# Scaling of q and v moved to the front of GpSimd's work of a step, in a retention layer fused with an x - tanh(x) feed-forward block

## The chip, the cores and the metric

One Trainium2 chip, one of its cores. The metric is the device time of the kernel in microseconds (us), as the median of several runs. Before the change it is 703.7 us (8 runs, 703.37 to 704.32).

## The reference

```python
# attention: q, k, v are (4, 8, 768, 64) f32
gamma = 1.0 - 2.0 ** (-5.0 - np.arange(H, dtype=np.float32))
scale = 1.0 / np.sqrt(D)
for t in range(S):
    state = gamma[None, :, None, None] * state + np.einsum('bhd,bhe->bhde', k[:, :, t], v[:, :, t])
    y[:, :, t] = scale * np.einsum('bhd,bhde->bhe', q[:, :, t], state)
# bridge: (B, H, S, D) -> x of (3072, 512)
# feed-forward: w_in (512, 2048), w_out (2048, 512), float64 as handed in
h = x @ w_in
g = h - np.tanh(h)
out = (g @ w_out).astype(np.float32)
```

## The kernel before, in words

**Attention by chunks.** The 3072 tokens are 24 chunks of 128. The decay gamma is taken out of the recurrence: q is multiplied by gamma^t / sqrt(D) and v by gamma^-t (`scale`, L262, one multiplication of 128x512 each, in place), so that a chunk needs only masked scores and a running state. A chunk ci passes through these pieces:

- `load_chunk` (L245): SP issues the loads of k, q and v, 256 KB each, in this order.
- `scale` (L262): q (which = 0) and v (which = 1).
- `turn_by_dma` (L300 to L305): ScalarE copies k and then the scaled q into `apart`, with the halves of each word apart; a DMA from ScalarE's queue writes that to `rows` in DRAM (L303); a transposing DMA on SP's queue reads it back as `kqT` (L305).
- `products` (L325, L331): PE's state products k, v and scores kqT. Then `mask` (L338) and `state` (L348 to L354) on VectorE.
- `outputs` and `outputs_rest` (L379): PE's y; `see` (L409) and `keep_x` (L425): ScalarE reads it and stores it as xT, the feed-forward's input.

**Feed-forward by steps.** The list `steps` has 96 entries (n, m2): a tile of 256 tokens by 256 hidden columns. Steps are called here by their place in it, from 0. In a step PE makes h (`up`, L444), ScalarE and VectorE make g = h - tanh(h) (`shrink_*`, L454 to L503), and PE multiplies g by w_out (`down`, L511) two steps later, so that h's two banks and the o banks are handed on from step to step. Where a run of steps on the same tokens ends, VectorE or ScalarE adds o into the sum (`add_up`, L521, L525), which frees the o bank for the next run. From step 32 on (n >= 4) a step uses a scheme with fewer products (`fast_up`, L758; `fast_products`, L649), which needs sums of weights and of tokens made ahead by GpSimd: `up_weights` (L738), `up_tokens` (L748), `fast_weights` (L590); and in each of these steps GpSimd adds pairs (`up_pairs`, L768) which VectorE uses in L773.

**Weights.** They come as 64-bit words and are turned into f32 by `convert`: two operations on ScalarE (L177, L178), four on VectorE (L186 to L192), and two on GpSimd (L200 `low` times `power`, L204 the sum, which writes w1 or w2). The buffers of `head`, `low` and `power` are double; `raw` has three.

**What sets the order.** The pools make the buffers, but the order of each engine's work is that of the program text: every engine, SP's queue too, runs its instructions in the order in which the loop issues them. Up to step 7 the order is a list written out by hand (`order`), and the change doesn't touch it. From step 8 the loop below runs. Two of three steps hold a chunk step (`with_chunk`); where it `falls_back` it stands behind that step's `up`. A chunk step ci does products of chunk ci + 2, loads chunk ci + 4 and turns chunk ci + 3 by DMA. `with_weights` gives steps 8 to 26 a conversion (two in step 8), and `with_sums` gives steps 25 to 39 and some later ones their sums. The scaling of the chunk that the next step's chunk step turns is issued in the step ahead of it:

| step | PE starts it, us | chunk step ci | chunk scaled | conversion | sums |
|---|---|---|---|---|---|
| 9 | 99.07 | 5 | none | 14 | |
| 10 | 105.95 | none | 9 | 15 | |
| 11 | 112.93 | 6 | 10 | 16 | |
| 12 | 121.02 | 7, falls back | none | 17 | |
| 17 | 163.33 | 10 | 14 | 22 | |
| 25 | 231.81 | none | 19 | 30 | up_weights 0 |
| 26 | 238.79 | 16 | 20 | 31 | up_weights 1 |
| 27 | 247.86 | 17, falls back | none | none | up_weights 2 |
| 28 | 256.80 | none | 21 | none | up_weights 3 |
| 29 | 264.80 | 18 | 22 | none | up_weights 4 |
| 30 | 273.88 | 19, falls back | none | none | up_weights 5, first tokens |
| 31 | 283.05 | none | 23 | none | up_weights 6 and 7, tokens 5 |
| 32 | 290.03 | 20 | none | none | fast_weights 0 |

The pattern repeats every three steps: chunk scalings stand in steps 8, 10, 11, 13, 14, 16, 17, 19, 20, 22, 23, 25, 26, 28, 29 and 31, for chunks 8 to 23. In steps 11, 14, 17, 20, 23, 26 and 29 the chunk that is scaled is also loaded in the same step.

Of the kernel before, what the change touches and what calls it, by code (L numbers as in the profile page):

```python
# [31 lines left out]
def kernel(  # L32
# [25 lines left out]
    nc = tc.nc  # L58
# [147 lines left out]
    def convert(i):  # L206
        convert_begin(i)
        convert_bits(i)
        convert_end(i, nc.gpsimd)
# [38 lines left out]
    def scale(ci, which, engine):  # L248
        if ci >= NCH:
            return  # L250
        t, g = loaded[ci][1 + which], (gw if ci < WIDE else gq, gv)[which]
        out_ = t
        if which == 0 and ci < WIDE:
            if not wide:
                wide.append(mid.tile([P, 2, RUN, 2, D], F32, tag="apart", name="wide", bufs=1))
            out_ = loaded[ci][1] = wide[0][:, ci % 2]
            out_ = out_.rearrange("p r i d -> p i r d")
            t, g = (x.rearrange("p (i r) d -> p i r d", r=RUN) for x in (
                t, g[:, ts(ci % CPB, H)][:, :, None].to_broadcast([P, H, D])))
        else:  # L260
            g = g[:, ts(ci % CPB, H)][:, :, None].to_broadcast([P, H, D])
        engine.tensor_tensor(out_, t, g, op=ALU.mult)  # L262
# [51 lines left out]
    def products(ci):  # L314

        kh, _, vh = loaded[ci]
        kT, qT = (sides[ci][:, i] for i in range(2))
        sp = banks("t", f"s_{ci}")
        keep_busy(sp[:, 0, :P])
        scores[ci] = halves = sp.rearrange("p r (w n t) -> p r w n t", w=2, n=NP)  # L320
        for p in range(NP):
            for a in range(2):
                for i in range(2):
                    h, r = 2 * p + i, ds(D * a, D)
                    nc.tensor.matmul(halves[ds(D * i, D), a, 1, p], kh[r, h], vh[r, h],  # L325
                                     start=True, stop=True, skip_group_check=True)
        for p in range(NP):
            for a in range(2):
                for i in range(2):
                    r = ds(D * i, D)  # L330
                    nc.tensor.matmul(halves[ds(D * a, D), i, 0, p], kT[r, p, ts(a, D)],  # L331
                                     qT[r, p, ts(a, D)], start=True, stop=True,
                                     skip_group_check=True)

    def mask(ci):
        halves = scores[ci]
        m = mid.tile([P, 2, NP, D], F32, tag="a", name=f"a_{ci}")
        nc.vector.tensor_tensor(m, halves[:, :, 0],  # L338
                                causal[:, None, None, :].to_broadcast([P, 2, NP, D]),
                                op=ALU.mult)  # L340
        masked[ci] = m

    def state(ci):
        halves = scores[ci]
        j = ci % CPB
        if j == 0:
            states[ci] = mid.tile([P, 2, NP, D], F32, tag="state", name=f"state_{ci}", bufs=3)
            nc.vector.tensor_copy(states[ci][:, 1], halves[:, 0, 1])  # L348
        else:
            nc.vector.tensor_tensor(states[ci][:, 1], halves[:, 0, 1], states[ci][:, 0],  # L350
                                    op=ALU.add)
        if j < CPB - 1:
            nxt = mid.tile([P, 2, NP, D], F32, tag="state", name=f"state_{ci + 1}", bufs=3)
            nc.vector.tensor_tensor(nxt[:, 0], halves[:, 1, 1], states[ci][:, 1], op=ALU.add)  # L354
            states[ci + 1] = nxt
# [56 lines left out]
    def outputs_rest(ci):  # L412
        halfway.pop(ci)(False)
        loaded.pop(ci)

    def keep_x(ci):
        n, nj = divmod(ci, BLK)
        if n not in xT:
            for i in (1, 0) if n == 0 else (n,):
                xT[i] = xp.tile([P, NP, BLK * P], F32, tag="xT", name=f"xT_{i}")  # L420

        half = xT[n][:, :, ts(nj // 2, TH)].rearrange("p (n r) t -> p r n t", r=2)
        y = y_banks[:, ci % 2][:, :: 1 - 2 * (ci % 2)]
        for odd in range(2):
            nc.scalar.copy(out=half[:, :, :, ds(P * odd + D * (nj % 2), D)],  # L425
                           in_=y[:, :, :, odd::2])
# [39 lines left out]
    def shrink_factors(n, m2):  # L466
        u = shrinking[n, m2][0]
        if n < FAST_UP:
            shrink_factor(n, m2)
        large, q1 = work("large", 2), work("q1", 1)  # L470
        nc.scalar.activation(q1, u, AF.Square, bias=bias1, scale=math.sqrt(A))  # L471
        nc.scalar.activation(large, u, AF.Relu, bias=bias_m)  # L472
        shrinking[n, m2] += [q1, large]
# [15 lines left out]
    def shrink_last_factor(n, m2):  # L489

        hp = hps.pop((n, m2))
        q1 = shrinking[n, m2][3]
        g = gT[n, m2] = gp.tile([P, 2, TH], F32, tag="g", name=f"g_{n}_{m2}")
        dst = hp if n < FAST_UP else g.rearrange("p i t -> p (i t)")
        nc.vector.scalar_tensor_tensor(dst, in0=q1, scalar=A * C1, in1=hp, op0=ALU.add,  # L495
                                       op1=ALU.mult)
        shrinking[n, m2].append(dst)
# [264 lines left out]
    def up_take(n, m2):  # L762
        nc.scalar.copy(out=odd_room[0], in_=hps[n, m2])  # L763
# [106 lines left out]
    with_chunk = {h // 2: FIRST - 3 + i for i, h in enumerate(halves)}  # L870
# [28 lines left out]
    def middle():  # L899

        if before and len(shrinking[before]) == 2:
            shrink_factor(*before)
            shrink_third(*before)

    def chunk_step(ci):
        if ci >= FIRST:
            outputs_rest(ci)
            keep_x(ci)
        middle()
        if before:  # L910
            shrink_factors(*before)
            shrink_last_factor(*before)
        if FIRST <= ci + 2 < NCH:
            products(ci + 2)
            mask(ci + 2)
            state(ci + 2)
        load_chunk(ci + 4)
        if not before:
            turn_and_see(ci)
        elif FIRST <= ci + 1 < NCH - 1:  # L920
            outputs(ci + 1)

    def turn_and_see(ci):
        if ci + 3 < NCH:
            turn_by_dma(ci + 3)
        if FIRST <= ci + 1 < NCH - 1:
            if not before:
                outputs(ci + 1)
            see(ci + 1)

    for s in range(BEGUN, len(steps)):
        n, m2, first, last = steps[s]
        fast = n >= FAST_UP
        ci = with_chunk.get(s)

        falls_back = s == FALL or s in behind_up
        lag = LAG + int(s >= FALL)
        if ci is not None and not falls_back:
            chunk_step(ci)
        for i in with_weights.get(s, []):  # L940
            convert(i)
            load_weights(i + 3)
        if fast:
            fast_up(n, m2, (1, 5, 7, 6))
            up_take(n, m2)
        else:
            for i in range(2):
                up(n, m2, i)
        if falls_back and ci is not None:
            chunk_step(ci)  # L950
        if before and ci is not None:
            turn_and_see(ci)
        if ci == NCH - 2:
            outputs(ci + 1)
            see(ci + 1)
        waiting.append(steps[s])
        if fast:
            if before and ci is None:
                shrink_factors(*before)
                shrink_last_factor(*before)  # L960
            up_pairs()
            for make in with_sums.get(s, []):
                make()
            downs(lag, 0)
            fast_up(n, m2, (2, 3, 4))
            up_add(n, m2)
            shrink_begin(n, m2)
            if before:
                shrink_end(*before)
                if before[0] >= FAST:  # L970
                    fast_sums(*before)
            downs(lag, 1)
            end_some(1)
            shrink_two(n, m2)
            before = n, m2
            if s + 1 not in with_chunk:
                middle()
        else:
            shrink_begin(n, m2)
            shrink_factors(n, m2)  # L980
            shrink_multiply(n, m2)
            downs(lag)
            shrink_last_factor(n, m2)
            shrink_end(n, m2)
            for make in with_sums.get(s, []):
                make()
        if s + 1 in with_chunk:
            for which in range(2):
                scale(with_chunk[s + 1] + 3, which, nc.gpsimd)
    shrink_factors(*before)  # L990
    shrink_last_factor(*before)
    shrink_end(*before)
# [64 lines left out]
```

## Time and profile before

| | |
|---|---|
| median of 8 runs | 703.7 us |
| the profiled execution, device time | 703.7 us |
| its span in the profile | 701.9 us |
| granted TensorE clock | 0.999 of full |
| PE busy | 690.8 us |
| VectorE (DVE) busy | 520.2 us |
| ScalarE (ACT) busy | 432.8 us |
| GpSimd (POOL) busy | 353.7 us |
| scaling of q on GpSimd from 90 us on (L262) | 16 times, median 1042 ns |
| scaling of v on GpSimd from 90 us on (L262) | 16 times, median 1272 ns |
| L200 on GpSimd, in the whole run | 30 times, median 1278 ns |

How to read it. The span is what the profiler saw of the program; the device time holds what lies around it. An engine is busy while it works on an instruction; PE's ends are modelled. In the view of waits a line names the engine and instruction that stood idle, what ended its idle time, the total, how often and the longest. In the timeline a number in square brackets is the idle time ahead of an instruction and what ended it. The chain of work that ended last is followed back from the program's end, at each step to what released it; "issue" in it is time in which the engine waited for nothing that the profile shows.

### The profile page before, as it was taken

The page shows a single profiled execution, that of the slowest core. Times are in us where ns is not written, and L with a number is a line of the kernel's source. Part 1 is how long each engine was busy: PE and PEld are TensorE (multiplying, and loading weights), DVE is VectorE, ACT ScalarE, POOL GpSimd, SP SyncE. Part 2 cuts the span into 40 slices and gives each one's busy share as a digit, 9 for nine tenths or more (in the row PEclk, how much of TensorE's full clock was granted, in tenths as well). Part 3 has the DMA queues.
Part 4 walks back from the last instruction along what each step waited for, and adds up shares of the span by engine and source line. Part 5 has one row for each costly group of instructions (what it writes and reads, how often), then busy time and mean ns, then how long its engine had stood idle before and what let it go on. Part 6 is the DMA issues. An engine that isn't in the chain of part 4 may idle for free.

```text
span 701.9 us, 16649 instructions
## 1 busy us (share of the span) xinstructions
PE 690.8 (98%) x6602; PEld 579.3 (83%) x6602; DVE 520.2 (74%) x888; ACT 432.8 (62%) x818; POOL 353.7 (50%) x523
## 2 busy tenths in 40 slices
PE   7999999999999999999999999999999999999997
PEld 6886666677667667679999999999999999999996
DVE  4898878979889667676776677676686676776765
ACT  4677657776767675565556655555665555666553
POOL 1464444645445577768854453354453444544333
PEclk9999999999999999999999999999999999999999
DMA  7880437887877666510000000000000000000001
GB/s 211 247 253 28 134 96 206 227 227 185 228 212 187 152 161 185 164 51 1 1 1 16 16 1 16 16 1 31 1 1 31 1 1 31 2 15 16 1 16 46
DMA packets 119677, 59.96 MB, mean 85 GB/s; under 512 B 101808, under 2 KB 112688, under 8 KB 119600
## 3 DMA queue, kind: packets, MB, share of 16 engines
q1 hardware_dynamic: 117008, 50.21, 27.2%
q10 hardware_dynamic: 2592, 8.69, 3.2%
q8 instruction: 52, 0.85, 0.5%
q14 instruction: 25, 0.20, 0.1%
HBM read 35.83 MB, written 14.68 MB: 72 GB/s over the span
## 4 chain that ended last, share of the span: by engine, by line
PE 82%; DVE 5%; ACT 4%; POOL 3%; issue 2%; DMA 2%; SPq 1%; ACTq 0%; POOLq 0%; DVEq 0%
PE h L758 28%; PE o L511 12%; PE h L444 10%; PE fast_t L649 10%; PE y L649 8%; PE fast_o L649 8%; PE y L379 3%; PE s L331 1%; ACT apart L300 1%; PE s L325 1%; POOL low L200 1%; DMA raw<-in_moe_w_in_dram 1%; POOL fast_raw L738 1%; DMA kqT<-rows 1%; DVE g L503 1%
## 5 line engine op out<-in xcount | busy, mean ns | idle before, releaser
L600 POOL TENSOR_TENSOR s<-g 128x128 f32<-128x128 f32 x64 | 29.2, 457 | 191.9 <-DVE g L503 188.0
L457 ACT ACTIVATE th<-h 128x512 f32<-128x512 f32 x64 | 38.2, 597 | 141.3 <-DVE h L775 138.6
L511 PE MATMUL o<-w,g 128*128 128x512 f32 x256 | 116.0, 596 | 0.8 <-DVE sum L521 0.8
L444 PE MATMUL h<-xT,w 128*128 128x256 f32 x480 | 110.2, 382 | 0.0
L444 PEld LDWEIGHTS h<-xT,w 128*128 128x128 f32 x480 | 90.0, 190 | 20.6 <-issue 8.9
L503 DVE COPY_PREDICATED g<-large,th 128x512 f32<-128x512 int32 x96 | 86.2, 898 | 10.0 <-DVE g L502 0.5
L200 POOL TENSOR_TENSOR low<-low,power 128x512 f32<-128x512 f32 x30 | 38.6, 1288 | 107.1 <-DVE power L192 74.3
L511 PEld LDWEIGHTS o<-w,g 128*128 128x128 f32 x256 | 47.5, 190 | 48.5 <-issue 44.0
L758 PEld LDWEIGHTS h<-xT,w 128*128 128x128 f32 x512 | 76.8, 191 | 8.4 <-ACT fast_head L763 1.0
L482 DVE TENSOR_TENSOR th<-h,th 128x512 f32<-128x512 f32 x94 | 64.1, 682 | 22.6 <-ACT th L455 21.3
L758 PE MATMUL h<-xT,w 128*128 128x128 f32 x512 | 78.3, 275 | 0.2 <-ACT fast_head L763 0.2
L773 DVE TENSOR_TENSOR h<-h,fast_head 128x256 f32<-128x256 f32 x64 | 27.7, 432 | 67.0 <-PE h L758 65.9
L463 ACT ACTIVATE q<-u,tab 128x512 f32<-128x512 f32 x96 | 69.7, 726 | 1.8
L495 DVE SCALAR_TENSOR_TENSOR g<-q,h 128x512 f32<-128x512 f32 x64 | 44.0, 688 | 36.0 <-ACT q L471 34.5
L471 ACT ACTIVATE q<-u,tab 128x512 f32<-128x512 f32 x96 | 69.5, 724 | 0.0
L472 ACT ACTIVATE large<-u,tab 128x512 f32<-128x512 f32 x96 | 68.5, 714 | 0.0
L758 PE MATMUL h<-x,w 128*128 128x128 f32 x448 | 68.3, 275 | 0.0
L486 DVE SCALAR_TENSOR_TENSOR h<-q,h 128x512 f32<-128x512 f32 x94 | 64.8, 689 | 3.8 <-ACT q L463 3.8
L758 PEld LDWEIGHTS h<-x,w 128*128 128x128 f32 x448 | 59.0, 192 | 0.0
L763 ACT COPY fast_head<-h 128x512 f32<-128x512 f32 x64 | 37.5, 585 | 20.1 <-PE h L758 20.0
L502 DVE TENSOR_TENSOR g<-g,u 128x512 f32<-128x512 f32 x64 | 49.2, 768 | 0.0
L768 POOL TENSOR_TENSOR fast_head<-fast_head 128x256 f32<-128x256 f32 x64 | 46.8, 731 | 4.5 <-ACT fast_head L763 4.5
(195 smaller groups left out, 1479.3 us busy)
## 6 DMA issues: line engine op xcount, KB each, us to landing
rows<-apart ACTq DMA_DIRECT2D x16, 512.0 KB, 4.0
k<-in_k_dram SPq DMA_DIRECT2D x24, 256.0 KB, 4.0
v<-in_v_dram SPq DMA_DIRECT2D x24, 256.0 KB, 4.6
raw<-in_moe_w_out_dram SPq DMA_DIRECT2D x12, 512.0 KB, 4.2
out_dram<-sum SPq DMA_DIRECT2D x22, 256.0 KB, 2.0
q<-in_q_dram SPq DMA_DIRECT2D x16, 256.0 KB, 4.7
raw<-in_moe_w_in_dram SPq DMA_DIRECT2D x14, 256.0 KB, 3.9
raw<-in_moe_w_in_dram SPq DMA_DIRECT2D x28, 128.0 KB, 3.7
```

Source lines behind the costliest of these rows:

```text
L444: nc.tensor.matmul(hp, w1[:, c, ts(2 * m2 + i, P)], xT[n // 2][:, c, ts(n % 2, TH)], start=(i == 0 and c == 0), stop=(c == NC - 1), skip_g ...
L463: nc.scalar.activation(q0, shrinking[n, m2][0], AF.Square, bias=bias0)
L471: nc.scalar.activation(q1, u, AF.Square, bias=bias1, scale=math.sqrt(A))
L472: nc.scalar.activation(large, u, AF.Relu, bias=bias_m)
L482: nc.vector.tensor_tensor(th, hp, th, op=ALU.subtract)
L486: nc.vector.scalar_tensor_tensor(hp, in0=shrinking[n, m2][2], scalar=C0, in1=hp, op0=ALU.add, op1=ALU.mult)
L502: nc.vector.tensor_tensor(flat, src, u, op=ALU.mult)
L503: nc.vector.copy_predicated(flat, large.bitcast(I32), th)
L511: nc.tensor.matmul(o_p[j], gT[n, m2][:, i, ts(j, P)], w2[:, 2 * m2 + i], start=(first and i == 0), stop=(last and i == 1))
L649: nc.tensor.matmul(accs[n][k], left[k - 1], right, start=first and k in (1, 6, 7, 4), stop=last, skip_group_check=True)
L758: nc.tensor.matmul(hps[n, m2][:, ts(PLACE[k], P)], s_of[m2][k - 1][:, c], x_of[n][k - 1][:, c], start=(k == 1 and c == 0), stop=(c == 1), ...
L768: nc.gpsimd.tensor_tensor(odd_room[1], first[:, :2], first[:, 3:1:-1], op=ALU.add)
```

## The change

The two scalings of the chunk that the next step turns are issued right behind this step's chunk step (or, where it has none or falls back, as the first thing of the step), ahead of the conversion and of the sums; before they were the last thing of the step.

```diff
@@ -937,6 +937,9 @@
         lag = LAG + int(s >= FALL)
         if ci is not None and not falls_back:
             chunk_step(ci)
+        if s + 1 in with_chunk:
+            for which in range(2):
+                scale(with_chunk[s + 1] + 3, which, nc.gpsimd)
         for i in with_weights.get(s, []):
             convert(i)
             load_weights(i + 3)
@@ -984,9 +987,6 @@
             shrink_end(n, m2)
             for make in with_sums.get(s, []):
                 make()
-        if s + 1 in with_chunk:
-            for which in range(2):
-                scale(with_chunk[s + 1] + 3, which, nc.gpsimd)
     shrink_factors(*before)
     shrink_last_factor(*before)
     shrink_end(*before)
```

Each engine but GpSimd has the same instructions in the same order as before; on GpSimd the pairs of L262 stand ahead of L200, L204, L738 and L748 of their step.

## The prediction

> **What bounds the kernel now.** First the busy shares of the page, then who waits for whom on PE from 40 to 330 us (which holds every step that the edit touches), then PE's timeline, then the chain of work that ended last.
>
> ```profile
> PE 690.8 (98%) x6602; PEld 579.3 (83%) x6602; DVE 520.2 (74%) x888; ACT 432.8 (62%) x818; POOL 353.7 (50%) x523
> ```
>
> PE is busy 690.8 of 701.9 us, so an edit on GpSimd (POOL) can pay only by what PE waits. These are all its waits in that stretch (us in total, times, longest):
>
> ```profile
> PE s L331 <- DMA kqT<-rows: 1.0, 1, 1.0
> PE o L511 <- DVE sum L521: 0.8, 1, 0.8
> PE y L379 <- DVE state L348: 0.3, 1, 0.3
> PE h L758 <- ACT fast_head L763: 0.2, 1, 0.2
> ```
>
> The third lies before 92 us, ahead of the edit. The other three in PE's timeline would be at 126.26, 261.17 and 308.16; the first two are these, in steps 12 and 28:
>
> ```profile
> 126.26 0.69 PE L331 MATMUL s<-kqT 64*64 64x64 f32 x32 [1.00 <-DMA kqT<-rows]
> ...
> 261.17 3.70 PE L511 MATMUL o<-w,g 128*128 128x512 f32 x8 [0.75 <-DVE sum L521]
> ```
>
> The chain says what stands behind the first (start, us, what); the q is chunk 9's:
>
> ```profile
> 113.66 1.28 POOL low L200
> ...
> 116.25 1.05 POOL q L262
> ...
> 117.32 1.05 ACT apart L300
> ...
> 118.39 3.62 DMA rows<-apart
> ...
> 122.03 4.18 DMA kqT<-rows
> ...
> 126.26 0.69 PE s L331 x32
> ```
>
> and behind the second, with chunk 20's q after the sums of up_weights (L738):
>
> ```profile
> 254.43 0.72 POOL fast_raw L738
> ...
> 255.15 1.01 POOL q L262
> ...
> 256.19 1.06 ACT apart L300
> ...
> 258.10 0.60 ACT u L454
> ...
> 259.22 0.69 DVE th L482
> ```
>
> Both go through the moved instruction: q is scaled last, ACT's copy of it (L300) waits, and all that ACT has behind it is late. ACT's waits from 90 to 300 us give the total, six waits:
>
> ```profile
> ACT apart L300 <- POOL q L262: 14.4, 6, 3.7
> ```
>
> **What the two waits really cost.** [...] I compare step lengths. Step 12 runs on PE from 121.02 to 131.12, 10.10 us; step 15, alike but for 16 more y matmuls (150.73 to 151.01, 0.28), from 147.18 to 156.35, 9.17. So 10.10 - (9.17 - 0.28) = 1.21 us. Step 28, 256.80 to 264.80, is 8.00; step 22, the same work, 206.58 to 213.56, is 6.98: 1.02 us. Together 2.23 us, where the idle marks say 1.75.
>
> [...] L503 takes 0.73 alone and 1.55 at 173.89 under the q scaling of 173.80, and the v scaling behind it takes 1.51 where 1.04 is its length alone.
>
> **The change, part by part.** Nothing is added or removed: 16 times q (1.04 us) and v (1.04 to 1.5) move ahead of that step's conversion (L200 and L204, 1.28 + 1.27, with about 2.6 from start to end) and sums. No DMA is issued by them and no queue is reordered; SP's list is the same.
>
> Step 10, chunk 9. GpSimd ended conversion 14 at 110.77. Its q load was issued at 101.51; q loads take 4.0 to 6.2 us, so it is there by 107.7. q is then scaled by 111.9, not 117.3. ACT's copy of k starts at 112.98 by ACT's own order, that of q then at 113.95, not 117.32: rows goes out 3.4 us earlier, at 115.0. Its landing (2.6 to 5.3 us) falls at 117.6 to 120.3; SP issues the transposing load after v of chunk 10, at 117.74 or later, and it takes 4.2 to 5.1: kqT is there at 122.0 to 125.4, likeliest (3.6 and 4.2) 122.8. PE wants it at 126.26 - 1.21 = 125.05. Gain 1.21, at worst 0.9.
>
> Step 26, chunk 20. GpSimd is free at 243.06; q's load, issued at 240.31, lands by 244.3 to 246.5; q is done by 247.6, and ACT wants it at 253.5. ACT's wait of 2.65 us goes whole. u, th, L482, L486 and the first L521 (260.43) come 2.65 earlier, at 257.8; PE's o result is there at 256.8. PE wants the bank at 261.17 - 1.02 = 260.15. Gain 1.02, covered by 1.7 us or so.
>
> The other four waits of ACT (3.7, 0.9, 0.7, 3.2 us) end in no PE wait: worth nothing.
>
> What goes behind q and v. In steps 11, 14, 17, 20, 23, 26 and 29 the load is issued in the same step, so GpSimd now stands waiting for it with the conversion queued behind. Step 17: v issued at 165.39, scaled by 173.5 at the latest, L200 2.3 us later than its 171.20, the weights at 176.1; PE wants them in step 19, at 184.80. The nearest case is conversion 31 in step 26: v issued at 240.88, 4.3 to 6.3 us to land, 1.04 to 1.5 to scale: L200 by 248.7, weights by 251.3 (251.68 now), wanted at 253.26 - 1.21 = 252.05. Cost 0, covered by 0.7 us at the worst end. ACT's next use of the head and low buffers is two conversions on: a whole step of cover.
>
> Steps 29 to 32. q of chunk 22 started at 271.31 and v at 273.48, on their loads; 265.79 to 269.30 was up4. Now up4 waits behind v: 3.5 us later. The 1.33 us that GpSimd waited at 285.95 is filled. So it is through with step 31 at 293.18 + 3.5 - 1.33 = 295.35, and up_pairs of step 32 is 0.5 us later than here:
>
> ```profile
> 294.87 0.72 POOL L768 TENSOR_TENSOR fast_head<-fast_head 128x256 f32<-128x256 f32 x1 [1.68 <-ACT fast_head L763]
> ```
>
> VectorE uses it at 297.33, when PE's h is there: 297.33 - 294.87 - 0.72 = 1.7 us of cover. Cost 0; without that cover it is one for one.
>
> Meeting on SBUF. q and v stretch other VectorE operations than before. Now a scaling costs L503 and the next L186 about 0.8 each; after, the loads' arrival decides. I take no difference; bounds -1.6 (no more meetings) and +1.8 us of VectorE in each of the 13 steps that scale and convert (rival D). VectorE is idle 39.5 of 200 us from 92 to 292, and g is ready well ahead (step 21's at 210.65, used at 219.20), which hides it.
>
> Sum: -1.21 - 1.02 = -2.2 us. The profiled execution took 703.7 us with a span of 701.9, and 703.7 is also the median of the eight runs: 703.7 - 2.2 = 701.5.
>
> **Rivals.**
> A. The forecast, 701.5; its own range 701.1 (the third wait, 308.16, goes too: step 34 would gain 0.3) to 702.1 (only the idle marks count).
> B. One wait stays. For: rows now runs beside the loads of chunk 10, and 125.4 is past 125.05; against: that needs both slowest landings. 703.7 - 1.0 to 1.2 = 702.6.
> C. It doesn't do what it says: PE's waits move to the next thing that is just late, and none of 2.2 us comes out: 703.7. For: the chain has DVE and ACT pieces too. Against: 3.4 and 2.65 us of relief for needs of 1.2 and 1.0.
> D. Slower: [...] q now falls on L186 to L192 (the conversion's SBUF operations), and pushes L200 and L204 from under VectorE's PSUM operations (L482 to L502, 2.8 us) onto L503. [...] From 92 to 240 VectorE has 148 - 127.7 = 20.3 us idle; half of it is usable at best when its inputs come in fixed order, plus 8.5 us of lead in g: 18.6. It decides from (18.6 + 2.2) / 13 = 1.6 us more VectorE a step, the gain eaten first. At 1.8, a hit by each of L200 and L204 more than now, it is 23.4 - 18.6 = 4.8 us of PE, less 2.2 gained: 703.7 + 2.6 = 706.3. Against: 1.6 is already paid a step now, and it goes when q moves.
>
> **How the numbers follow.** A 0.62, B 0.15, C 0.09, D 0.14. A measurement here tells about 0.2% (1.4 us) from none, that is below 702.3 or above 705.1. A is faster, B and C are the same, D is slower: faster 0.62, same 0.24, slower 0.14. The range 701.0 to 703.9 holds A (its end of 701.1 and what the median wavers), B and C, and leaves out D.
>
> **What would show it.** Right: no wait of L331 for kqT in step 12 and none of L511 for L521 in step 28; those steps 8.9 and 7.0 us long on PE; ACT's waits for q near 0; rows of chunk 9 out 3 us earlier; GpSimd idle before q, for its load; up_pairs of step 32 about 0.5 us later against PE. Wrong: a new PE wait for L204, for L773 or for g, or VectorE's L503 and L186 to L192 in sum over 1.4 us longer a step.

## The result and the profile after

The median after is 701.86 us (12 runs, 701.33 to 703.01), before 703.71 (32 runs): ratio 0.9974, 95% interval 0.9967 to 0.9981. The profiled execution took 701.78 us with a span of 700.0, against 703.7 and 701.9. The forecast was 701.5.

The page of the kernel after, busy shares:

```profile
PE 691.6 (99%) x6602; PEld 580.5 (83%) x6602; DVE 523.1 (75%) x888; ACT 432.6 (62%) x818; POOL 355.4 (51%) x523
```

PE is busy 0.8 us more than before (its ends are modelled) and the span is 1.9 us shorter, so the gain is idle time of PE. What PE still waits for, from 40 us on (us in total, times, longest):

```profile
PE h L758 <- ACT fast_head L763: 0.2, 1, 0.2
```

L331's wait and L511's wait are gone, and so is the 0.3 of L348, which lies at 50.95, ahead of the edit. PE's timeline at steps 12 and 28 (start, us, what):

```profile
120.92 3.62 PE L444 MATMUL h<-xT,w 128*128 128x256 f32 x16
124.46 0.69 PE L325 MATMUL s<-v,k 64*64 64x64 f32 x32
125.17 0.69 PE L331 MATMUL s<-kqT 64*64 64x64 f32 x32
...
130.03 2.32 PE L444 MATMUL h<-xT,w 128*128 128x256 f32 x10
```

```profile
255.72 3.62 PE L444 MATMUL h<-xT,w 128*128 128x256 f32 x16
259.17 3.60 PE L511 MATMUL o<-w,g 128*128 128x512 f32 x8
262.70 0.46 PE L379 MATMUL y<-a,v 64*64 64x64 f32 x16
```

Step 12 lasts 130.03 - 120.92 = 9.11 us (10.10 before), step 28 262.70 - 255.72 = 6.98 (8.00 before). From the first h of step 9 to the first h of step 32 it is 98.97 to 290.01, 191.04 us, against 99.07 to 292.12, 193.05: 2.01 less, which is the whole gain. This stretch, called the stage below, is what I compare between kernels: the first h of step 9 comes at 98.2 to 100.9 us in the fourteen profiled executions of this document, and the edit begins only in step 8. Steps 13 to 27 and 29 to 31 agree with those of before to 0.03 us.

The chain of work that ended last, at the place where it held `low`, q, `apart`, `rows` and `kqT` before:

```profile
121.08 3.45 PE h L444 x16
124.53 0.62 PE s L325 x32
125.16 0.01 issue
125.17 0.69 PE s L331 x32
```

It is PE alone now. ScalarE's six waits for q (14.4 us) are gone. Here the two copies of chunk 9 follow one another:

```profile
112.32 1.04 ACT L300 COPY apart<-k 128x1024 uint16<-128x1024 uint16 x1
113.25 1.05 ACT L300 COPY apart<-q 128x1024 uint16<-128x1024 uint16 x1
114.33 0.34 ACTq L303 DMA_DIRECT2D rows<-apart  x1
```

On GpSimd the scalings stand ahead of conversion 15, and v, not q, waits for its load:

```profile
107.69 1.03 POOL L262 TENSOR_TENSOR q<-q,tab 128x512 f32<-128x512 f32 x1
109.06 1.13 POOL L262 TENSOR_TENSOR v<-v,tab 128x512 f32<-128x512 f32 x1 [0.33 <-DMA v<-in_v_dram]
112.27 1.28 POOL L200 TENSOR_TENSOR low<-low,power 128x512 f32<-128x512 f32 x1 [2.08 <-DVE power L192]
```

That q starts at 107.69 is already more than the forecast had: conversion 14 ends at 107.73 here and not at 110.77. Something ahead of chunk 9 has moved as well; the experiments take this up.

### The profile page after: what moved, and what is told of

The parts are those of the page before. It is cut to its first block, busy times and chain, and to the rows that moved or that the text cites. A ratio compares the mean times of both kernels' runs of the same rounds, so it can differ in the third digit from the quotient of the medians.

```text
span 700.0 us, 16643 instructions
## 1 busy us (share of the span) xinstructions
PE 691.6 (99%) x6602; PEld 580.5 (83%) x6602; DVE 523.1 (75%) x888; ACT 432.6 (62%) x818; POOL 355.4 (51%) x523
## 4 chain that ended last, share of the span: by engine, by line
PE 94%; DVE 2%; issue 1%; ACT 1%; SPq 1%; DMA 0%; POOL 0%; POOLq 0%; DVEq 0%; ACTq 0%
PE h L758 28%; PE o L511 16%; PE h L444 15%; PE fast_t L649 10%; PE y L649 8%; PE fast_o L649 8%; PE y L379 3%; PE s L331 1%; PE s L325 1%; PE kqTp L276 1%; PE h_early L444 1%; PE kqTp L217 1%; PE h_early L217 1%; DMA k<-in_k_dram 0%; SPq L159 0%
## 5 line engine op out<-in xcount | busy, mean ns | idle before, releaser
L511 PE MATMUL o<-w,g 128*128 128x512 f32 x256 | 115.9, 595 | 0.0
L503 DVE COPY_PREDICATED g<-large,th 128x512 f32<-128x512 int32 x96 | 80.0, 833 | 9.7
L511 PEld LDWEIGHTS o<-w,g 128*128 128x128 f32 x256 | 47.6, 190 | 47.4 <-issue 44.7
L482 DVE TENSOR_TENSOR th<-h,th 128x512 f32<-128x512 f32 x94 | 64.1, 682 | 20.3 <-ACT th L455 19.0
L773 DVE TENSOR_TENSOR h<-h,fast_head 128x256 f32<-128x256 f32 x64 | 27.7, 433 | 68.3 <-PE h L758 65.6
L463 ACT ACTIVATE q<-u,tab 128x512 f32<-128x512 f32 x96 | 69.6, 725 | 1.8
L200 POOL TENSOR_TENSOR low<-low,power 128x512 f32<-128x512 f32 x30 | 39.3, 1309 | 55.8 <-DVE power L192 44.2
L763 ACT COPY fast_head<-h 128x512 f32<-128x512 f32 x64 | 37.5, 585 | 19.2 <-PE h L758 19.0
L502 DVE TENSOR_TENSOR g<-g,u 128x512 f32<-128x512 f32 x64 | 48.6, 759 | 0.0
```

The source lines that it names most:

```text
L463: nc.scalar.activation(q0, shrinking[n, m2][0], AF.Square, bias=bias0)
L482: nc.vector.tensor_tensor(th, hp, th, op=ALU.subtract)
L502: nc.vector.tensor_tensor(flat, src, u, op=ALU.mult)
L503: nc.vector.copy_predicated(flat, large.bitcast(I32), th)
L511: nc.tensor.matmul(o_p[j], gT[n, m2][:, i, ts(j, P)], w2[:, 2 * m2 + i], start=(first and i == 0), stop=(last and i == 1))
```

## The experiments

The first theory is the forecast's: each PE wait hangs on one chunk's own q, step 12's on chunk 9's and step 28's on chunk 20's, and the other fourteen moves are worth nothing. The rival theory spreads the gain: fewer meetings of GpSimd and VectorE on SBUF in all the steps that scale. What a meeting is worth is read from the trace of before, from 92 to 292 us: L503, whose tiles are all in SBUF, takes 0.73 to 0.75 us with no GpSimd operation beside it (7 times) and 0.82 to 1.57 where one overlaps it by over 0.25 us (16 times), while L482 to L502, which read h from PSUM, take 0.67 to 0.70 with and without one. What makes L503 longer was not shown. The kernels of the first two groups differ from the one before in a single condition. Their common edit stands here:

```diff
         if ci is not None and not falls_back:
             chunk_step(ci)
+        moved = with_chunk[s + 1] + 3 if s + 1 in with_chunk else NCH
+        early = ...
+        if early:
+            for which in range(2):
+                scale(moved, which, nc.gpsimd)
         for i in with_weights.get(s, []):
...
-        if s + 1 in with_chunk:
+        if not early:
             for which in range(2):
-                scale(with_chunk[s + 1] + 3, which, nc.gpsimd)
+                scale(moved, which, nc.gpsimd)
```

### Which chunks carry it: four kernels

Chunk 9 alone:

```diff
+        early = moved == 9
```

> Only the scaling of chunk 9 (step 10) is moved to the front. Theory 1 (the two PE waits hang on q coming late to ScalarE): the wait of step 12 goes, that of step 28 stays: 703.7 - 1.0 = 702.7 us, PE's waits from 92 us on are L511 for L521 (0.75) and L758 (0.2). Theory 2 (VectorE meets GpSimd less often on SBUF, a little in each of the 16 scalings): 1/16 of the gain, 703.6.

Chunk 20 alone:

```diff
+        early = moved == 20
```

> Only the scaling of chunk 20 (step 26) is moved to the front. Theory 1: the wait of step 28 goes, that of step 12 stays: 702.7 us, PE's wait is L331 for kqT (1.0). Theory 2: 703.6.

All but these two:

```diff
+        early = moved not in (9, 20)
```

> All scalings are moved but those of chunks 9 and 20, the two whose q stands right ahead of PE's waits. If a wait hangs on its own chunk's q alone: both stay, 703.7 us. If the wait of ScalarE for the q of the chunk ahead (8 and 19, 3.7 and 3.2 us) is handed on through the conversion of the next step, then q of 9 and 20 come some 1.4 and 2.4 us earlier in their old place too, and both waits are gone or nearly so: 701.7 to 702.2. Theory 2: 14/16 of the gain, 701.95, but with both waits of PE still there.

All but these two and the one before each:

```diff
+        early = moved not in (8, 9, 19, 20)
```

> All scalings are moved but those of chunks 8, 9, 19 and 20. Theory 1, in both forms: both PE waits stay (1.0 and 0.75) and the other twelve are worth nothing: 703.7 us. Theory 2: 12/16 of the gain: 702.2.

The four ran beside a kernel before that took 705.02 us at the median (58 runs, 703.61 to 709.08), and this chip's times scatter more than the others' (702.76 to 705.39 for the same kernel). Step lengths are from the profiled executions; "10.10 and 10.09" are those of before (for step 28 from first h to first h, which takes in the start of step 29).

| kernel | median, us | ratio to before, 95% | step 12 | step 28 | stage |
|---|---|---|---|---|---|
| before | 705.02 | | 10.10 | 10.09 | 193.05 |
| chunk 9 | 704.84 | 0.9997, 0.9987 to 1.0007 | 10.16 | 9.89 | 193.58 |
| chunk 20 | 703.63 | 0.9976, 0.9968 to 0.9985 | 10.45 | 9.07 | 193.86 |
| all but 9, 20 | 702.63 | 0.9968, 0.9956 to 0.9981 | 9.20 | 9.07 | 192.48 |
| all but 8, 9, 19, 20 | 705.20 | 0.9995, 0.9982 to 1.0009 | 9.97 | 10.07 | 192.92 |

The first theory fails for step 12. Chunk 9 alone doesn't remove its wait, and without chunk 9 it goes. For step 28, chunk 20 alone is enough, yet the wait also goes without it. The rival theory fails too: the twelve other moves together bring nothing that is clear of noise (at best 1.3 us by the interval, where the rival asks for 1.5; 0.13 us in the stage), and PE's two waits stand in that kernel as before:

```profile
PE s L331 <- DMA kqT<-rows: 0.9, 1, 0.9
PE o L511 <- DVE sum L521: 0.7, 1, 0.7
```

The medians of chunk 20 and of "all but 9, 20" are better than their stages say; the profiled execution was in both the slowest of its kernel and had late `kqT` loads elsewhere (0.53 and 0.49 us of PE waiting in the one, 0.97 at 190.82 in the other). Smaller ones stand in other kernels too (0.31 at 190.63 with chunk 9 alone), and no run shows their cause. I rest on the steps here, not on these two medians.

Why does chunk 9's move not help on its own? Its q was scaled at 111.73 to 112.77 and ScalarE didn't wait for it (its copy ran at 114.94), as forecast. But the q scaling met VectorE's L503, and the v scaling met L186 of conversion 15:

```profile
111.82 1.57 DVE L503 COPY_PREDICATED g<-large,th 128x512 f32<-128x512 int32 x1
113.27 1.26 DVE L186 TENSOR_SCALAR head<-head 128x512 f32<-128x512 f32 x1
```

Before, at this place, they took 0.75 and 0.42 us, so the conversion's last VectorE operation ends 1.6 us later. That conversion's `raw` buffer is what SP's weight loads wait for. SP's queue with chunk 9 alone:

```profile
110.95 7.00 SPq L159 DMA_DIRECT2D raw<-in_moe_w_in_dram  x6
...
119.47 2.23 SPq L245 DMA_DIRECT2D v<-in_v_dram  x1
121.79 3.49 SPq L305 DMA_TRANSPOSE kqT<-rows  x1
```

and before (this execution is 1.01 us earlier at step 12):

```profile
110.19 4.62 SPq L159 DMA_DIRECT2D raw<-in_moe_w_in_dram  x6
...
116.30 1.44 SPq L245 DMA_DIRECT2D v<-in_v_dram  x1
122.03 1.81 SPq L305 DMA_TRANSPOSE kqT<-rows  x1
```

Before, SP has issued v by 117.74 and then stands for `rows` until 122.03. With chunk 9 alone the six weight loads take 7.00 us and not 4.62, so v is issued by 121.70 and the transposing load right behind it: `rows`, which ScalarE sent 3.4 us earlier against its step (116.04 - 1.01 against 118.39), isn't what it waits for any more. Against its step the transposing load is still issued 1.25 us earlier than before (121.79 - 1.01 against 122.03), about what PE needed. But it lands 5.50 us later where before it took 4.18, and PE waits as long as ever. The chain behind this wait no longer holds ScalarE's copy or `rows`:

```profile
113.27 1.27 DVE head L186
...
117.69 1.28 POOL w L204
118.97 0.45 SPq L245
...
119.47 2.23 SPq L245
...
121.79 5.50 DMA kqT<-rows
```

```profile
127.33 0.69 PE L331 MATMUL s<-kqT 64*64 64x64 f32 x32 [1.06 <-DMA kqT<-rows]
```

The longer landing is not an accident of one execution. This load of chunk 9 landed in 5.0 to 6.0 us in six kernels that issue it ahead of step 12's first h (the change, chunk 9, chunk 8, chunks 8 and 19, all but 9 and 20, q first and v last), and in 4.2 to 4.3 us in the five that issue it behind that (before, chunk 20, chunk 19, all but 8, 9, 19 and 20, and the kernel before with fillers). Why it takes longer when it goes early, no run separates.

How SP hangs on conversion 15 is read from the trace. SP's weight loads wait for L190, the last reader of `raw`, before and with chunk 9 alone:

```profile
SPq L159 <- DVE head L190: 1.0, 1, 1.0
```

```profile
SPq L159 <- DVE head L190: 2.6, 1, 2.6
```

The chain above reaches SP by way of L204 instead, which belongs to the same conversion. That one of these is the link is argued, not shown: no kernel with a fourth `raw` buffer was run.

### The chunk ahead: three kernels

The theory that is left, already named in the expectation for all but 9 and 20: ScalarE's wait for one chunk's q is handed on, through what ScalarE has behind it, to the next chunk. Chunk 8's q, late in step 9 (before: 3.66 us, ScalarE's longest), holds up conversions 14 and 15, and with them GpSimd's way to chunk 9's q and SP's weight loads; chunk 19's does the like for 20.

```diff
+        early = moved == 8
```

> Only the scaling of chunk 8 (step 8) is moved. Theory H (handed on): ScalarE's wait of 3.66 us for q of chunk 8 is what makes conversions 14 and 15 late, and with them both q of chunk 9 on GpSimd and the loads ahead of kqT on SP's queue; the wait of PE in step 12 goes, though chunk 9 stays where it was: 1.0 us less than before, PE's waits are L521 (0.75) and L763 (0.2). Theory O (own chunk): the wait of step 12 stays.

```diff
+        early = moved == 19
```

> Only the scaling of chunk 19 (step 25) is moved. Theory H: conversion 31 and the sums of step 26 come about 1.5 us earlier, q of chunk 20 behind them too, ScalarE's copy of it no longer waits more than 1 us, and PE's wait in step 28 goes: 1.0 us less than before, with L331 for kqT (1.0) left. Theory O: the wait of step 28 stays.

```diff
+        early = moved in (8, 19)
```

> Only the scalings of chunks 8 and 19 are moved. Theory H: the whole gain of the change, 2.0 us less than before, with only the wait of L758 for L763 (0.2) left on PE from 92 us on. Theory O: nothing, both waits stay.

Beside a kernel before of 703.79 us (40 runs):

| kernel | median, us | ratio to before, 95% | step 12 | step 28 | stage |
|---|---|---|---|---|---|
| chunk 8 | 703.45 | 0.9999, 0.9991 to 1.0007 | 9.16 | 10.05 | 192.78 |
| chunk 19 | 702.65 | 0.9986, 0.9979 to 0.9992 | 10.13 | 9.07 | 192.06 |
| chunks 8 and 19 | 702.62 | 0.9978, 0.9970 to 0.9987 | 9.30 | 9.07 | 191.23 |

Each removes the wait that was named for it and no other. Chunk 8 alone: ScalarE's copies of q of chunk 8 and of chunk 9, and PE's use:

```profile
98.73 1.05 ACT L300 COPY apart<-q 128x1024 uint16<-128x1024 uint16 x1
...
113.55 1.05 ACT L300 COPY apart<-q 128x1024 uint16<-128x1024 uint16 x1 [0.94 <-POOL q L262]
```

```profile
123.72 0.69 PE L325 MATMUL s<-v,k 64*64 64x64 f32 x32
124.46 0.69 PE L331 MATMUL s<-kqT 64*64 64x64 f32 x32
```

Chunk 9's q is still last on GpSimd, but ScalarE waits 0.94 us for it and not 3.27, since conversion 15 comes 2.9 us earlier against its step (its L200 at 109.88 against 113.66, with the step itself 0.85 earlier). With chunk 19 alone, q of chunk 20 is likewise in its old place, at 252.15, and ScalarE, at 253.81, no longer waits for it. In the profiled execution of chunk 8's kernel, the fastest of its thirteen, two small waits for `kqT` further on (steps of 9.40 and 9.55 us where 9.06 and 9.18 stood) take 0.71 us of the gain back. Its median shows no gain (at best 0.6 us by the interval), and by the medians chunks 8 and 19 together are not told from chunk 19 alone; that step 12's wait hangs on chunk 8 rests on the traces. There it holds throughout. Over all fourteen profiled executions, those of the groups below with them, step 12 lasts 8.87 to 9.30 us in the eight kernels that move chunk 8 and 9.97 or more in the six that don't, whatever chunk 9 does. Step 28, from first h to first h, lasts 9.06 to 9.40 us in the nine kernels that move chunk 19 or 20 and 9.89 or more in the other five.

Two chunks of sixteen thus bring 1.82 of the 2.01 us of the stage. In step 12 they leave 0.2 us that the change's own execution doesn't have; but two further kernels below have the change's text up to step 25, and there step 12 takes 8.87 and 9.20 us where the change took 9.11, so differences of that size are not read as effects.

### The order of q and v

The q of a chunk goes ahead of the conversion, its v stays last:

```diff
+        moved = with_chunk[s + 1] + 3 if s + 1 in with_chunk else NCH
+        scale(moved, 0, nc.gpsimd)
         for i in with_weights.get(s, []):
...
-        if s + 1 in with_chunk:
-            for which in range(2):
-                scale(with_chunk[s + 1] + 3, which, nc.gpsimd)
+        scale(moved, 1, nc.gpsimd)
```

> q is moved to the front of all 16 steps, v stays last. If only q counts: 2.0 us less than before, as the whole change; GpSimd no longer waits for v ahead of the conversions, and up_pairs of step 32 stands closer to its place before than the change has it (1.1 us later against PE). If the meetings of v with VectorE on SBUF count: a part of the gain is missing.

It took 701.68 us, ratio 0.9968 (0.9956 to 0.9980), stage 190.80, step 12 8.88: 0.24 us less than the change in the stage and 2.25 less than before, where the forecast's two waits sum to 2.23. The medians of the two don't tell them apart. So nothing of the gain hangs on moving v. The 0.23 us by which step 12 is shorter here isn't shown to come from the order, since step 12 varies as much between executions of the same text (8.87 to 9.20 us). In the change's own run `kqT` is issued at 119.40 and takes 5.7 us to land, at 125.1, where PE would have wanted it a little earlier (its L331 starts 0.71 us after L325 there, and 0.51 in this kernel).

### Taking the cover away: three kernels

Three edits put operations of 112 columns on GpSimd whose result nobody uses, to see whether what the forecast called hidden is hidden by what it named. The line numbers of these kernels are higher by 5 from L106 on.

```diff
+    pad = cst.tile([P, 112], F32, name="pad")
+    def fill(n):
+        for _ in range(n):
+            nc.gpsimd.tensor_tensor(pad, tab[:, :112], tab[:, :112], op=ALU.mult)
```

To the changed kernel, seven behind the sums of step 31:

```diff
+            if s == FIRST_UP - 1:
+                fill(7)
```

> The change, with seven idle GpSimd operations (112 columns, about 0.42 us each, 2.9 us in all) at the end of step 31, ahead of up_pairs of step 32. up_pairs ends 0.63 us ahead of its use by VectorE (L773) in the changed kernel. One for one beyond that: 2.3 us more than the change, in PE waits of steps 33 and 34. By the trace of the change ScalarE has another 1.3 us idle behind L773 (ahead of L763 at 298.72): about 1.0 us more than the change. If up_pairs is not on a path to PE: no difference.

To the changed kernel, twelve ahead of conversion 31:

```diff
+        if s == 26:
+            fill(12)
         for i in with_weights.get(s, []):
```

> The change, with twelve such operations (5.0 us in all) between v of chunk 20 and conversion 31 in step 26. In the changed kernel the weights of conversion 31 are ready at 250.2 and PE wants them at about 253.0 (the second of the matmuls from 252.18 on): 2.8 us of cover. One for one beyond it: step 27 grows from 8.94 to 11.1 us, PE waits 2.2 us in L511 for L204, 2.2 us more than the change. If the conversion has more cover than that: no difference.

To the kernel before, three ahead of chunk 9's q:

```diff
+        if s == 10:
+            fill(3)
         if s + 1 in with_chunk:
             for which in range(2):
```

> The kernel before, with three such operations (1.26 us in all) right ahead of q of chunk 9 in step 10. If PE's wait in step 12 hangs on that q: one for one, the wait of L331 for kqT grows from 1.0 to 2.3 us, step 12 from 10.10 to 11.4, 1.3 us more than before. If it hangs on SP's queue alone (loads of chunk 10 ahead of kqT): less than 0.5 us.

Beside a kernel before of 703.67 us (25 runs) they took 704.64 (1.0013, 1.0001 to 1.0025), 705.38 (1.0036, 1.0022 to 1.0050) and 707.06 (1.0050, 1.0035 to 1.0066).

In step 31 the fillers took 3.09 us, 0.44 each (the 0.42 of the expectation was an estimate); `up_pairs` of step 32 came 3.8 us later against PE than in the change, and VectorE then waited for it. PE's waits there:

```profile
PE y L384 <- ACT xT L430: 1.5, 1, 1.5
PE h L763 <- ACT fast_head L768: 0.5, 1, 0.5
```

From the first h of step 32 to the h that waits for L763 in step 34 PE took 17.90 us (291.12 to 309.02), against 16.05 in the change (290.01 to 306.06): 1.85 more, for 3.8 less 0.63 of cover. Expected were 2.3, or 1.0 if all of ScalarE's idle time counts. So the cover is real and it ends where VectorE's L773 stands; what lies beyond it is passed on by rather more than half.

In step 26 the weights of conversion 31 came 2.4 us too late for PE (2.2 was expected):

```profile
257.15 4.24 PE L516 MATMUL o<-w,g 128*128 128x512 f32 x6 [2.40 <-POOL w L209]
261.19 3.95 PE L449 MATMUL h<-xT,w 128*128 128x256 f32 x16
```

Ahead of chunk 9's q the three fillers took 1.62 us, and the wait of L331 grew by 1.40 (2.40 where 1.00 was), nearly one for one. So a later q costs PE at once, although an earlier q alone gains nothing: there SP and the longer landing take the gain back. But both kernels lost more than PE's wait. Step 27 of the one took 12.96 us where 11.1 was expected, step 12 of the other 13.17 where 11.4 was. In the first the six o products took 4.04 us to the next instruction and the h behind them 3.79, where the same h take 3.45 in the change. In the second, after L331's wait, the eight o products took 5.21:

```profile
127.91 0.69 PE L336 MATMUL s<-kqT 64*64 64x64 f32 x32 [2.40 <-DMA kqT<-rows]
...
129.24 5.38 PE L516 MATMUL o<-w,g 128*128 128x512 f32 x8
134.45 1.89 PE L449 MATMUL h<-xT,w 128*128 128x256 f32 x8
```

The change has 3.54 for those eight (126.49 to 130.03). The cause is in the granted clock. These are stretches of the kernel before with fillers (bounds and length, then the busy us of PE, PEld, DVE, ACT and POOL, each with its count in brackets, then the clock, the DMA share and GB/s); the clock is the figure behind the last bracket:

```profile
121.00:128.00 7.00, 4.61 (x54) 3.54 (x56) 6.19 (x10) 7.00 (x13) 4.23 (x4) 1.00 0.66 177
128.00:130.00 2.00, 2.00 (x81) 1.67 (x82) 1.93 (x3) 1.30 (x6) 0.78 (x1) 0.81 0.78 260
130.00:132.00 2.00, 2.00 (x4) 0.71 (x3) 1.93 (x5) 2.00 (x4) 1.14 (x1) 0.50 0.74 229
132.00:134.50 2.50, 2.50 (x7) 1.10 (x6) 2.36 (x5) 1.89 (x4) 1.42 (x2) 0.87 1.03 302
134.50:145.00 10.50, 10.50 (x160) 7.67 (x159) 8.15 (x15) 5.54 (x11) 4.55 (x4) 1.00 0.86 177
```

The clock falls to half and comes back: 2.00 x 0.19 + 2.00 x 0.50 + 2.50 x 0.13 = 1.70 us lost. In the other kernel it is 0.61 from 258 to 260 and 0.54 from 260 to 262, 2.00 x 0.39 + 2.00 x 0.46 = 1.70 us as well.

### One wait that was left

The change's last PE wait after 60 us, in step 34, is for ScalarE's L763. To the kernel with q first and v last, L763 goes ahead of the L463 that stands before it in that step:

```diff
             fast_up(n, m2, (1, 5, 7, 6))
             up_take(n, m2)
+            if s == FALL + 1:
+                middle()
...
-            if s + 1 not in with_chunk:
+            if s + 1 not in with_chunk and s != FALL:
                 middle()
```

> q first and v last, as in the run before, and in step 34 ScalarE's copy L763 stands ahead of L463, which in step 33 was issued at the end and now after the copy. PE's last wait from 92 us on, L758 for L763 in step 34 (0.18 us marked, some 0.3 in the step's length), goes: 0.3 us less than with q first alone, so 2.5 us less than before. If L463 later makes L486 and g late: the wait comes back in step 35 or 36.

It took 701.81 us, 0.9971 (0.9960 to 0.9982). PE then waits for nothing from 60 to 330 us, and the stretch from the wait's group of h to the next takes 3.51 us (302.37 to 305.88) where the change has 3.85. The 0.34 us are seen in the trace and not in the median.

## Why the prediction was right, and where its reason failed

**The sum.** -2.2 us was forecast; the stage shows -2.01, the profiled executions 703.7 - 701.78 = 1.9, the medians 1.85. Rival A came, within its own range. B, C and D did not: both waits went, and nothing took their place. But the sum held with help from a part that it had put at nothing, as step 10 shows.

**What a wait costs.** Step lengths against a like step gave 1.21 and 1.02 us where the idle marks sum to 1.75. The kernel with q first and v last, which has neither wait, measures 2.25. The step lengths were right.

**Step 10, chunk 9: the step that failed.** The prediction let the gain come from chunk 9's own q ("q is then scaled by 111.9, not 117.3 ... rows goes out 3.4 us earlier"). Every time in it came true in the kernel that moves chunk 9 alone, up to `rows`, and the wait stayed. Three things were taken from the trace of before as if fixed.

The first is SP: "SP issues the transposing load after v of chunk 10, at 117.74 or later". That time hangs on conversion 15, which the moved q and v scalings stretch: with chunk 9 alone SP came to the transposing load at 121.79, 3.0 us later against its step. The second is the landing: "it takes 4.2 to 5.1". It took 5.50 us there and 5.7 in the change. The third is "The other four waits of ACT (3.7, 0.9, 0.7, 3.2 us) end in no PE wait: worth nothing". Chunk 8's wait of 3.66 us is the head of the chain: with it gone, step 12's wait goes even with chunk 9 in its old place.

In the change both move, and there luck comes in. The landings of `rows` (the least figure) and of `kqT` (the greatest) in the change:

```profile
DMA to landing us min/median/max: 5.1/5.4/5.7
```

These are the two slow landings that rival B asks for. With them, `rows` sent at the forecast's 115.0 would have put `kqT` at 115.0 + 5.1 + 5.7 = 125.8, and at 125.1 even with the shortest of the early landings, 5.0: an estimate, 0.05 to 0.75 us past the need of 125.05. `rows` went out at 114.33, and `kqT` was there at 125.1. So the forecast's 2.2 us of margin (122.8 against 125.05) was not there, and what brought `rows` out earlier than forecast and SP to its load in time was the move of chunk 8, which the forecast had priced at nothing.

**Step 12's size.** 0.99 in place of 1.21, inside the stated "at worst 0.9": `kqT` came about 0.2 us after PE wanted it.

**Step 26, chunk 20.** Right as a way, but not the only one. L521 starts at 256.59 after the change, 2.76 us earlier against its step (2.65 forecast), and step 28 is 6.98 as forecast. Chunk 20 alone does it, and chunk 19 alone does it as well, since ScalarE is then no longer late when it comes to chunk 20.

**What goes behind q and v.** Cost 0, right. Conversion 31 in the change, with the q ahead of it, which waits for its load:

```profile
244.02 1.23 POOL L262 TENSOR_TENSOR q<-q,tab 128x512 f32<-128x512 f32 x1 [1.14 <-DMA q<-in_q_dram]
...
248.56 1.63 POOL L204 TENSOR_TENSOR w<-low,head 128x512 f32<-128x512 f32 x1
```

L200 of that conversion, whose last input VectorE ended at 245.54 (L192), came at 247.22, right behind v: GpSimd kept the order of the text. The weights are there at 250.19 (251.3 was the forecast's worst; with its own latest q, done by 247.6, v would follow only by 249.1 and the weights by 251.7, so its worst case had 0.4 us of cover and not 0.7). The kernel with twelve fillers shows what the cover was: beyond it PE waits 2.40 us for L204.

**Steps 29 to 32.** `up_pairs` of step 32:

```profile
293.88 0.72 POOL L768 TENSOR_TENSOR fast_head<-fast_head 128x256 f32<-128x256 f32 x1
```

It is 293.88 - 287.93 = 5.95 us into the step (PE's start of it), and 294.87 - 290.03 = 4.84 before: 1.1 later, where 0.5 was forecast, so 0.6 mis-sized. VectorE uses it at 295.23, which leaves 0.63 of the 1.7 us of cover. Part of the difference is a wait of 1.07 us for the load of chunk 23's q in step 31, which the forecast doesn't have. The price stayed 0.

**Meetings on SBUF.** "No difference" was right for PE: VectorE's whole busy time rose from 520.2 to 523.1 us, 2.9 us over 13 steps or 0.2 a step, far below the 1.6 from which rival D decides; its 1.8 was my assumption, not a measured figure. The meetings moved, from L503 (mean 898 to 833 ns) to the operations of the conversion (from 92 to 292 us, means: L186 588 to 707 ns, L188 475 to 642, L190 741 to 831, L192 427 to 614). What the prediction didn't see is that such meetings can make a conversion late (1.6 us with chunk 9 alone) and SP's queue behind it.

## What to carry to other kernels

When an engine waits several times in a row for the same kind of thing, the wait that hurts need not be caused by the item it is for: ask what the wait before it delayed, and move one item at a time to find out. A time in the trace of before at which a queue gets to an instruction is itself a result of waits (here on the weights' conversion), and the time that a load takes to land may change with the moment of its issue (4.2 to 4.3 us late, 5.0 to 6.0 early, here); before resting on either, ask what sets it and whether the edit moves that. Size a wait of PE by the length of its step against a like step, and compare executions by the length of the stage that was edited, since an unrelated part may vary by as much as the gain. Compare steps of several executions of the same text before reading 0.2 us as an effect.

## What the runs showed of the hardware that was not expected

In two profiled executions, of different kernels and in different steps, a PE wait of 2.40 us cost 1.70 us more than its length: the granted clock went to half behind it (0.50 and 0.54 in the worst stretches of 2 us) and was full again within 7 us of the wait's end. Behind three shorter waits no such fall was measured. In step 12 before, with 1.00 us, the clock is 1.00 in every stretch from 121 to 135 us. In the kernel with seven fillers, with 1.53 us, it is 1.00 in every stretch from 300 to 312 us. With chunk 20 alone step 12 has a wait of 1.34 us, 0.34 more than before, and is 0.35 us longer, so nothing came on top there.

Not every execution of a kernel shows it. A loss of 1.70 us takes 0.002 off the mean clock of such a run. The kernel with twelve fillers in step 26 ran twelve times: in four executions, the profiled one among them, the mean clock was 0.994 to 0.997 and the time 706.55 to 709.29 us; in the other eight it was 0.999 or 1.000, and seven of these took 704.31 to 705.45. How long PE waited in the executions that were not profiled isn't known, and no wait between 1.53 and 2.40 us was measured. For this change it means that a lateness which lets a PE wait grow to 2.40 us may cost more than its length, 1.70 us on top in these two executions; the wait of 1.00 us that the change removed paid no such price.
